# Band mask of the softmax maximum on VectorE, and the softmax reciprocals spread by DMA

## The chip, the cores and the metric

The kernel runs on one core of a Trainium2 chip. The profile calls the core's engines PE (TensorE, matmuls; PEld is its weight loads), DVE (VectorE), ACT (ScalarE), POOL (GpSimd) and SP (SyncE, which here issues almost every DMA). Each engine works through its own instruction list in order and waits on semaphores for the others. The metric is the device time of one execution in microseconds.

## The reference

Two independent results are computed and put side by side: a sliding-window attention on the left 576 columns, a long convolution (a state-space kernel, done by FFT) on the right 576.

```python
def _A_ref(x, wqkv, wo):                      # x: 1 x 2048 x 576
    H = 32; Dh = 18; W = 256
    q, k, v = ...                             # x @ wqkv, 32 heads of 18
    scores = jnp.einsum("bhqd,bhkd->bhqk", q, k) * (Dh ** -0.5)
    idx = jnp.arange(S)
    mask = (idx[:, None] - idx[None, :] >= 0) & (idx[:, None] - idx[None, :] < W)
    scores = jnp.where(mask[None, None], scores, -1e9)
    p = _softmax(scores, axis=-1)
    return (p @ v per head, heads joined) @ wo

def _B_ref(u, A_re, A_im, B_re, B_im, C_re, C_im, log_dt, Dskip):
    K = ...                                   # 576 kernels of length 2048 from 128 complex modes
    return causal_convolution(u, K) + u * Dskip
```

Only the attention's softmax is touched by the change.

## The kernel before

The program has three stages. Up to about 402 us the projections to q, k and v and the tables of the convolution's kernels are computed. From 402 to about 790 us the attention runs, with the convolution's spectra and inverse transforms mixed in. The rest is mostly the output projection.

The attention is cut into 16 *items*: four chunks of 512 queries by four groups of eight heads. An item passes through these steps, each a generator that yields its pieces:

- `smax`: for each of 8 blocks of 64 queries and two halves of the heads, a PSUM tile of 128 rows x 2 x 320 gets the scores of the block against the 320 keys that its window can touch (L836, four matmuls on the four quarters of the array). Four more matmuls (L844, or L847 where the window begins before the sequence does) multiply an identity by the constant `sm`, whose entries are 0 or -3e38, and so add the mask to the first and the last 64 keys. VectorE takes the maximum over each 320 (L870, one reduction of 128x640 to 128x2). Sixteen such tiles make an item's maxima; they are transposed (L852), halved to fp16 (L856) and stored by four small DMAs (L863, Q<-m) as an additional row of Q.
- `scores` computes the scores again with keys on the partitions, less the maximum (L921), masks them (L930), and ScalarE takes the exponential (L936).
- `pv` multiplies by V (L956). V carries a 19th column of constants, so that of each group of 32 partitions the rows 0 to 17 hold a head's output and row 18 holds the softmax's denominator. ScalarE copies the result to SBUF as `osb` (L966).
- `norm` turns row 18 into its reciprocal on all rows: VectorE transposes `osb` in 32x32 blocks (L981), takes the reciprocal of one column (L983), and transposes that column, repeated 32 times, back (L985). GpSimd multiplies (L990), ScalarE and GpSimd split the product into two fp16 parts (L994, L998), SyncE stores them (L1003, od<-oh). The output projection (L178) later reads them.

All tiles of TensorE in this stage, of attention and convolution alike (L675 and L708 are the convolution's spectra and inverse, L769 its last transform, L690 and L691 its products on VectorE), share a *ring* of three PSUM slots. A slot is free when the engine that reads the tile has finished.

The order of the work is written out by hand as a string, `PLAN`. A letter asks the generator of that name for its next piece (s for smax, a for scores, v for pv, n for norm, c and d for the convolution's spectra and inverse); a letter with a digit runs the oldest piece that the generator has posted under that digit, such as s2, the reduction of the oldest finished tile. The string sets the order on every engine at once, and on SyncE's queue.

## Time and profile before

| quantity | value |
|---|---|
| median of 3 runs | 883.62 us (881.54 to 885.16) |
| profiled execution: time | 884.13 us |
| profiled execution: span | 882.3 us |
| granted TensorE clock, mean | 0.922 |
| VectorE, maximum's reductions (L870) | 187.7 us in 256 instructions |
| VectorE, transposes (L981, L985), 16 each | 19.8 and 19.9 us |
| TensorE, mask matmuls of the maximum (L844, L847) | 56.9 and 6.8 us in 1024 instructions |

Times in the profile are microseconds from the start of the span unless they are marked ns. A row of the grouped view names line, engine, operation, output <- inputs, shapes and count, then the busy time, the mean length of one in ns, the engine's idle time just before, and which work ended that idle time. A row of the chain view is a start, a length and the work that held the path; it is followed back from the last instruction to what released it. A row of the waits view gives the total, the number and the longest of one kind of wait. The busy time of matmuls includes their passage through the array, so matmuls that overlap are counted by their union, and a busy TensorE need not be at its peak.

### The profile page before, as it was taken

The numbers are of one execution on the slowest core, as the hardware profiler recorded it, in microseconds if no ns is written. First come the engines' busy times: TensorE is split into PE (matmuls) and PEld (weight loads), VectorE is DVE, ScalarE is ACT, GpSimd is POOL, SyncE is SP. The second block draws the span as 40 slices with busy tenths as digits, with TensorE's granted clock in tenths as the row PEclk, the third lists the DMA queues.
The fourth block names the chain that finished last, engine by engine and source line by source line (L and its number), as shares of the span: only waits on it lengthen the run. The fifth ranks groups of instructions, "written<-read, shape, count | busy, mean of one in ns | idle before, by whom it ended". The sixth has DMA issues, their size and how long they took to land.

```text
span 882.3 us, 32024 instructions
## 1 busy us (share of the span) xinstructions
PE 724.2 (82%) x14234; PEld 440.0 (50%) x14234; DVE 599.7 (68%) x798; ACT 522.7 (59%) x685; POOL 378.0 (43%) x295
## 2 busy tenths in 40 slices
PE   4565957998889789886888888887998987999977
PEld 2321523456446545454555554455555554567655
DVE  5855887887987787768657796575876767861010
ACT  3247676678777857671455566555766666676421
POOL 2256867766687655665015142221332042432020
PEclk9885969999999999996889999869999999999998
DMA  9795261546247745458549667637639573846743
GB/s 310 256 230 137 61 160 34 141 100 175 63 106 199 152 116 161 99 158 233 145 147 293 212 212 232 163 103 240 204 120 270 166 227 116 264 144 181 236 143 129
DMA packets 211051, 150.85 MB, mean 171 GB/s; under 512 B 102698, under 2 KB 191530, under 8 KB 210656
## 3 DMA queue, kind: packets, MB, share of 16 engines
q1 hardware_dynamic: 208896, 144.80, 58.5%
q0 software_dynamic: 2016, 3.99, 1.5%
q8 instruction: 112, 1.84, 0.9%
q14 instruction: 27, 0.22, 0.1%
HBM read 83.50 MB, written 65.11 MB: 168 GB/s over the span
## 4 chain that ended last, share of the span: by engine, by line
PE 46%; DVE 17%; ACT 12%; issue 10%; DMA 6%; SPq 4%; POOL 4%; ACTq 0%; DVEq 0%; POOLq 0%
PE pp L178 9%; PE po L956 7%; PE ring L178 6%; DVE m L870 5%; ACT P L936 4%; PE ring L708 4%; PE ring L921 4%; PE ring L836 3%; PE ring L675 3%; PE ring L575 2%; PE ring L453 2%; PE ring L769 2%; PE ring L465 2%; DMA K<-kz 1%; DVE m L552 1%
## 5 line engine op out<-in xcount | busy, mean ns | idle before, releaser
L870 DVE TENSOR_REDUCE m<-ring 128x2 f32<-128x640 f32 (+4 forms) x256 | 187.7, 779 | 66.6 <-PE ring L844 61.5
L936 ACT ACTIVATE P<-ring,esc 128x1024 f32<-128x1024 f32 (+2 forms) x160 | 166.8, 1060 | 102.3 <-PE ring L930 91.7
L546 POOL TENSOR_TENSOR m<-A,tr 128x1024 f32<-128x1024 f32 x72 | 144.0, 2017 | 79.2 <-DVE m L552 66.7
L956 PE MATMUL po<-P,V 64*32 64x320 f32 (+4 forms) x2816 | 105.7, 369 | 6.3 <-issue 6.3
L836 PE MATMUL ring<-K,Q 54*64 54x320 f16 (+4 forms) x1024 | 82.3, 322 | 26.5 <-DMA K<-kz 8.6
L696 POOL TENSOR_TENSOR Y<-t,t 128x384 f32<-128x384 f32 x24 | 24.0, 998 | 139.2 <-DVE t L691 133.3
L990 POOL TENSOR_TENSOR osb<-osb,T 128x1024 f32<-128x1024 f32 x16 | 37.8, 2362 | 100.6 <-DVE T L985 80.9
L921 PE MATMUL ring<-Q,K 55*64 55x320 f16 (+4 forms) x1408 | 67.7, 270 | 14.1 <-ACT P L936 3.4
L836 PEld LDWEIGHTS <-Q 54*64 54x64 f16 x1024 | 42.8, 109 | 71.7 <-issue 63.4
L998 POOL TENSOR_TENSOR oh<-osb,oh 128x1024 f16<-128x1024 f32 x16 | 34.1, 2130 | 73.5 <-ACT oh L994 73.5
L178 PE MATMUL pp<-xh,wh 128*128 128x512 f16 x180 | 48.6, 401 | 19.0 <-ACT vst L365 9.6
L178 PEld LDWEIGHTS <-wh 128*128 128x128 f16 x324 | 31.7, 101 | 57.1 <-issue 17.6
L844 PE MATMUL ring<-sm,idb 64*64 64x128 bf16 x896 | 56.9, 229 | 1.5 <-issue 1.5
L552 DVE TENSOR_TENSOR m<-m,m 128x1024 f32<-128x1024 f32 x36 | 53.3, 1480 | 4.8 <-POOL m L546 4.7
L956 PEld LDWEIGHTS po<-P,V 64*32 64x32 f32 x2816 | 39.1, 108 | 34.5 <-issue 25.0
L575 PE MATMUL ring<-Q,m 128*32 128x64 f32 x2304 | 42.6, 231 | 16.1 <-DVE m L552 13.4
L921 PEld LDWEIGHTS <-K 55*64 55x64 f16 x1408 | 33.8, 110 | 42.7 <-issue 34.0
L575 PEld LDWEIGHTS ring<-Q,m 128*32 128x32 f32 x2304 | 37.0, 117 | 29.8 <-issue 12.6
L178 PE MATMUL pp<-xh,wl 128*128 128x512 f16 x180 | 49.9, 412 | 0.0
L981 DVE STREAM_TRANSPOSE T<-osb 128x1024 f32<-128x1024 f32 x16 | 19.8, 1235 | 42.7 <-ACT osb L966 42.7
L930 PE MATMUL ring<-tm,idb 64*64 64x128 bf16 (+1 forms) x1152 | 44.9, 213 | 2.9 <-issue 2.9
L527 POOL TENSOR_TENSOR tr<-tr,mab 128x768 f32<-128x768 f32 x18 | 33.6, 1867 | 31.2 <-ACT tr L522 31.1
(162 smaller groups left out, 1570.2 us busy)
## 6 DMA issues: line engine op xcount, KB each, us to landing
gx<-ust SPq DMA_DIRECT2D x16, 576.0 KB
gk<-kst SPq DMA_DIRECT2D x18, 512.0 KB
tx<-gx SPq DMA_DIRECT2D x24, 384.0 KB
tk<-gk SPq DMA_DIRECT2D x24, 384.0 KB
h<-ho SPq DMA_DIRECT2D x48, 192.0 KB
hp<-h SPq DMA_DIRECT2D x12, 768.0 KB
Q<-qz SPq DMA_DIRECT2D x16, 512.0 KB
K<-kz SPq DMA_DIRECT2D x16, 512.0 KB
```

Of the source, the lines that this page charges most:

```text
L178: self.nc.tensor.matmul(ps, u, v, start=(i == 0), stop=(i == len(ops) - 1))
L546: tt(m[part], A[:, ch, a0:a0 + 8].unsqueeze(3).to_broadcast(sh), tr[:, ch, part, 0:8].unsqueeze(2).to_broadcast(sh), op=OP.mult)
L552: self.nc.vector.tensor_tensor(m[0], m[0], m[1], op=OP.add)
L575: nc.tensor.matmul(kp[32 * st:32 * st + 32, j, :], m[:, ch, 32 * term:32 * term + 32], Q[:, ch, term, :], start=(term == 0), stop=(term == ...
L836: nc.tensor.matmul(ps[z:z + 64, b, :n], d["Q"][rr, 2 * b + pp, 64 * qb:64 * qb + 64], d["K"][rr, 2 * b + pp, k0:k1], start=True, stop=Fals ...
L844: nc.tensor.matmul(out, self.idb[rr], self.sm[rr], start=False, stop=True, skip_group_check=True)
L870: self.nc.vector.tensor_reduce(out, x, axis=AX.X, op=OP.max)
L921: nc.tensor.matmul(ps[z:z + 64, b, off:off + w], d["K"][rr, 2 * b + pp, kc:kc + 64], d["Q"][rr, 2 * b + pp, q0:q0 + w], start=(k == 0), st ...
L930: nc.tensor.matmul(ps[z:z + 64, b, 64 * blk:64 * blk + w], self.idb[rr], self.tm[rr, self.MO[kinds]:self.MO[kinds] + w], start=False, stop ...
L936: nc.scalar.activation(P[:, :, lo:hi], ps[:, :, lo:hi], AF.Exp, scale=self.esc)
L956: nc.tensor.matmul(po[32 * p:32 * p + 32, z, q0:q0 + w], V[64 * z:64 * z + 64, kb * 76 + 19 * p:kb * 76 + 19 * p + 32], P[p % 2][64 * z:64 ...
L990: nc.gpsimd.tensor_tensor(osb, osb, rb, op=OP.mult)
```

## The change

Two parts of the softmax are moved.

First, the mask of the maximum. The mask matmuls L844 and L847 are gone. The constant `sm` grows from 128 to 320 columns, with zeros in the middle, and VectorE adds it while it takes the maximum: per tile two passes over 320 elements in place of one reduction over 640. A pass writes the masked scores to a scratch tile that nothing reads, and a second instruction writes the accumulated maximum.

Second, the reciprocals of the items 0 to 13. A DMA takes row 18 of the four groups of `osb` into a 128x32 tile R (step n); VectorE takes its reciprocal (n5); a DMA stores it to DRAM (n7); four DMAs load it back, one row to 18 partitions each (n8), into one tile `rb` that all items share. GpSimd then multiplies as before (n3). Items 14 and 15 keep the transposes.

In `PLAN`, only steps of n are moved or added: n, which now issues a DMA, stands 1 to 98 steps earlier than the transposes stood; n5 comes 10 to 12 steps behind it, n7 two steps later, n8 seven or eight later still (18 once), and n3 where it was or, for four items, 7 to 38 steps later. All other letters keep their order.

```diff
-    sm = np.concatenate([np.where(x <= p, big, 0), np.where(x > p, big, 0)], 1)
+    sm = np.concatenate([np.where(x <= p, big, 0), np.zeros((64, 192)), np.where(x > p, big, 0)], 1)
...
-        "a1vc2asaa1a1s6Lavva1sc3aa1ss2s2svs2ss4saa1s2s2ssas2s2sa1kss2s2nvvn3aa1kcc1aa1dc2sad1s2sksvs2s2a1v1cc"
+        "a1nvc2asaa1a1s6Lavvn5a1sn7c3aa1ss2s2svn8s2ss4saa1s2s2ssas2s2sa1kss2s2vvn3aa1kcc1aa1dc2sad1s2sksvs2s2"
...
-        self.sm = ap.tile([128, 128], BF, name="sm")
+        self.sm = ap.tile([128, 320], BF, name="sm")
...
+        self.rden = self.p["dram"].tile([self.LR, 4, 1024], F32, name="rden")
+        self.rb = ap.tile([128, 1024], F32, name="rb")
+        nc.gpsimd.memset(self.rb, 1.0)
...
                         nc.tensor.matmul(ps[z:z + 64, b, :n], d["Q"][rr, 2 * b + pp, 64 * qb:64 * qb + 64],
-                                         d["K"][rr, 2 * b + pp, k0:k1], start=True, stop=False, skip_group_check=True)
-                for b in range(2):
-                    for r in range(2):
-                        z = 64 * (r ^ b)
-                        rr = slice(64 * r, 64 * r + 64)
-                        if full:
-                            out = ps[z:z + 64, b, :320].rearrange("p (t x) -> p t x", x=64)[:, 0:5:4]
-                            nc.tensor.matmul(out, self.idb[rr], self.sm[rr], start=False, stop=True,
-                                             skip_group_check=True)
-                        else:
-                            nc.tensor.matmul(ps[z:z + 64, b, n - 64:n], self.idb[rr], self.sm[rr, 64:],
-                                             start=False, stop=True, skip_group_check=True)
-                self.post("2", (ps,), lambda out=mv[:, :, 8 * pp + qb], x=ps[:, :, :n]: self.red(out, x))
+                                         d["K"][rr, 2 * b + pp, k0:k1], start=True, stop=True, skip_group_check=True)
+                self.post("2", (ps,), lambda s=8 * pp + qb, x=ps[:, :, :n], m=m: self.red(m, s, x))
...
-    def red(self, out, x):
-        self.nc.vector.tensor_reduce(out, x, axis=AX.X, op=OP.max)
+    def red(self, m, s, x):
+        n = x.shape[2]
+        for b in range(2):
+            y = self.p["m"].tile([128, 320], F32, name="masked")
+            self.nc.vector.tensor_tensor_reduce(y[:, :n], x[:, b], self.sm[:, 320 - n:], 1.0, -3e38, op0=OP.add, op1=OP.max,
+                                                accum_out=m[:, 16 * b + s:16 * b + s + 1])
         self.n["max"] += 1
...
+            R = np_.tile([128, 32], F32, name="R")
+            if i < self.LR:
+                nc.sync.dma_start(R, osb.rearrange("(p r) z (k c) -> r p (z k) c", r=32, c=32)[18])
+                self.post("5", (R,), lambda i=i, osb=osb, R=R: self.spread(i, osb, R))
+                continue
             T = np_.tile([128, 32, 32], F32, name="T")
             nc.vector.transpose(T.rearrange("p k r -> p (k r)"), osb.rearrange("p z c -> p (z c)"))
-            R = np_.tile([128, 32], F32, name="R")
...
+    LR = 14
+
+    def spread(self, i, osb, R):
+        nc, rb, row = self.nc, self.rb, self.rden[i]
+        nc.vector.reciprocal(R, R)
+
+        def out():
+            nc.sync.dma_start(row.rearrange("p (k c) -> (p k) c", c=32), R)
+            self.post("8", (R,), back)
+
+        def back():
+            for p in range(4):
+                nc.sync.dma_start(rb[32 * p:32 * p + 18], row[p:p + 1].partition_broadcast(18))
+            self.post("3", (rb,), lambda: self.norm2(i, osb, rb.rearrange("p (z c) -> p z c", z=2)))
+        self.post("7", (R,), out)
```

What the string does to two instruction lists. First VectorE around the reciprocal of item 3, in the kernel before. Names are output <- inputs; t are the convolution's products, and what stands in brackets is the counter that the instruction waits for (PE_49, DVE_49, Activation_49 and Pool_49 count finished instructions of an engine, DMAHW numbers finished DMAs).

```order
L870 TENSOR_REDUCE m<-ring 128x2 [waits PE_49] x7
L981 STREAM_TRANSPOSE T<-osb 128x1024 [waits Activation_49,Pool_49]
L983 RECIPROCAL R<-T 128x32 [waits DVE_49]
L985 STREAM_TRANSPOSE T<-R 128x1024 [waits DVE_49]
L690 TENSOR_TENSOR t_7204<-X,ring 128x768 [waits PE_49,Activation_49,Pool_49]
L691 TENSOR_TENSOR t_7205<-X,ring 128x768
L870 TENSOR_REDUCE m<-ring 128x2 [waits PE_49] x4
```

The same place in the changed kernel, whose lines are numbered otherwise: L864 are the new passes (`ISA` is a masked maximum, or with m alone the write of the accumulated value), L991 is the reciprocal.

```order
L864 ISA masked,m<-ring,sm 128x320 [waits DVE_49,PE_49]
L864 ISA m 128x1
L864 ISA masked,m<-ring,sm 128x320 [waits DVE_49]
L864 ISA m 128x1
L991 RECIPROCAL R<-R 128x32 [waits DMAHW4_49,DMAHW1_49]
L691 TENSOR_TENSOR t_7118<-X,ring 128x768 [waits PE_49,Activation_49,Pool_49]
L692 TENSOR_TENSOR t_7119<-X,ring 128x768
L864 ISA masked,m<-ring,sm 128x320 [waits DVE_49,PE_49]
```

The first four rows stand for one reduction of before. The reciprocal keeps its place behind the run of reductions and ahead of the products, but waits for a DMA in place of VectorE's own transpose.

Second, SyncE's queue where the loads of item 5 are issued (Q_4396, K_4397 and V_4398 are that item's tiles, od the stores of finished items, tx and tk loads of the convolution). Before:

```order
L721 DMA h<-ho 128x2x192 x2
L806 DMA Q_4396<-qz 128x2048
L807 DMA K_4397<-kz 128x4x512
L809 DMA K_4397<-kz 128x4x256
L812 DMA V_4398<-vd 128x912
L660 DMA tx<-gx 128x4x192
L660 DMA tk<-gk 128x4x192
```

In the changed kernel:

```order
L722 DMA h<-ho 128x2x192 x2
L977 DMA R<-osb 128x1x32
L994 DMA rden<-R 128x32
L810 DMA Q_4396<-qz 128x2048
L811 DMA K_4397<-kz 128x4x512
L813 DMA K_4397<-kz 128x4x256
L816 DMA V_4398<-vd 128x912
L999 DMA rb<-rden 18x1024 x4
L661 DMA tx<-gx 128x4x192
L661 DMA tk<-gk 128x4x192
```

Six DMAs of item 2 have come in between: the read of the denominators and the store of the reciprocals ahead of the next loads, the four broadcast loads behind them.

More of the change, by code (lines that the diff above doesn't have):

```diff
@@ new lines @@
+        "vd4a1sss2d1n8akva1sd4s2s2vd4asc3a1s2dslld1s6kn6ss4sas2s2svs2a1ss2savs2ss2a1sas2vd4a1sass2n3s2va1ss2s"
+        "as2n1vsa1as2n6a1ss2ss2vLcllv1c1aaa1a1vvc2nss2ss2fakva1aa1sn5fan7vss6a1c3ee1s2n8saa1s2dcd1e4vvc1c2aav"
+        "vc3a1sa1s2s4aasfvs2kla1a1slvs2v1Ln4n4cc1c2elnsve1vs2ss2asa1s2sn5aa1n7ss2ss2asn3s2n8a1ss2s2ss2ss2svva"
+        "lc3s2cn1lla1c1aa1ad4vvc2n3ssa1ss6as2s2a1vss2as4ssve4a1s2ss2avs2asa1a1ds2svad1s2a1n6ssc3s2s2sas2sv1a1"
+        "vvaas2a1a1nss2vvdss2d1asn5ss2n7s2a1fvkkLcn8c1d4c2vaa1dd1sss6n4s2ass2va1aa1n3ess2ve1ss4s2ss2avn1ss2a1"
@@ L128 @@
+        "ww1w4aaa1vva1ee1e4ee1faavva1n3w4a1aa1www1wwwww4wwvvw1w4fn1n6w1vvv1ee4nn3w1e1w4wn1ee1n4ww4www1w4wn6n4"
+        "wwww1w4w1wwww4e4e4ww1ww4w1wwwww4w1w4w1w4ww1w4",
 }
```

34 lines of the change are left out of this document (13 added, 21 removed).

## The prediction

> **What bounds the kernel now.** I read the page's busy shares first, then busy time by stage, then the chain of waits in the stage that the change touches, then who waits for whom there. All terms below are set against the profiled execution: span 882.3 us, time 884.13 us, which is 0.06% above the median of 883.62 us. About 0.5% (4.4 us) is what a measurement of this kernel can tell from no change.
>
> ```profile
> span 882.3 us, 32024 instructions
> PE 724.2 (82%) x14234; PEld 440.0 (50%) x14234; DVE 599.7 (68%) x798; ACT 522.7 (59%) x685; POOL 378.0 (43%) x295
> core 0: us, PE busy (x) PEld busy (x) DVE busy (x) ACT busy (x) POOL busy (x), PEclk, DMA share, GB/s
> 0.00:402.00 402.00, 310.71 (x3704) 176.68 (x3704) 308.04 (x407) 260.99 (x407) 253.38 (x212) 0.91 0.57 149
> 402.00:790.00 388.00, 333.15 (x9498) 205.83 (x9501) 284.19 (x383) 227.03 (x238) 109.20 (x76) 0.93 0.66 193
> 790.00:882.30 92.30, 80.30 (x1048) 57.45 (x1032) 7.51 (x8) 34.73 (x41) 15.43 (x9) 0.96 0.56 172
> ```
>
> The change lies almost wholly in the middle row: from 402 to 790 us TensorE is busy 333 of 388 us (86%), VectorE 284 (73%). Neither fills the stage alone. The chain of waits over the same stretch says what holds it:
>
> ```profile
> by line: PE po L956 14.1%; DVE m L870 11.2%; ACT P L936 9.8%; issue 9.0%; PE ring L921 7.7%; PE ring L708 7.7%; PE ring L836 7.6%; PE ring L675 6.3%; PE ring L769 3.6%; DMA K<-kz 3.3%; DMA Q<-m 2.5%; PE ring L930 2.4%; PE ring L844 2.0%; SP
> ```
>
> TensorE's lines in it add up to 51%, the maximum's reduction (L870) has 11.2% of 388, 43.5 us, and the mask matmuls that go (L844) have 2.0%, 7.8 us. The coupling is the ring of three PSUM slots: TensorE may begin a tile only when the engine that empties the tile three before has done so.
>
> ```profile
> 649.53 3.10 DVE L870 TENSOR_REDUCE m<-ring 128x2 f32<-128x640 f32 x4 [0.64 <-PE ring L844]
> 651.96 0.41 PE L921 MATMUL ring<-Q,K 55*64 55x320 f16 x8 [0.28 <-DVE m L870]
> 652.69 0.33 PE L836 MATMUL ring<-K,Q 54*64 54x320 f16 x4 [0.23 <-DVE m L870]
> DVE m L870 <- PE ring L844: 61.5, 66, 5.0
> ```
>
> Here four reductions run back to back, and two tiles of TensorE start as each of the last two frees a slot. The last row says that VectorE sat idle for a fresh tile only 66 times, 61.5 us in all; the other reductions found their tile ready. So a longer reduction is passed on to TensorE in bursts, and a shorter matmul helps between them.
>
> **The change, part by part.** Rows for the prices:
>
> ```profile
> L870 DVE TENSOR_REDUCE m<-ring 128x2 f32<-128x640 f32 x224 | 174.4, 821 | 63.0 <-PE ring L844 61.5
> L474 DVE TENSOR_TENSOR fa<-ring,fa 128x384 f32<-128x384 f32 x18 | 10.0, 553 | 17.7 <-ACT fa L471 17.7
> L474 DVE TENSOR_TENSOR fr<-ring,fr 128x512 f32<-128x512 f32 x36 | 24.7, 685 | 15.9 <-ACT fr L471 15.5
> L162 DVE TENSOR_SCALAR or<-or 128x1 f32<-128x1 f32 x1 | 0.2, 154 | 0.0
> L985 DVE STREAM_TRANSPOSE T<-R 128x1024 f32<-128x1024 f32 x14 | 17.4, 1245 | 0.5
> L981 DVE STREAM_TRANSPOSE T<-osb 128x1024 f32<-128x1024 f32 x14 | 17.3, 1233 | 0.0
> 717.66 0.06 PE ring L844 x4
> 649.43 0.08 PE ring L844 x4
> 717.77 4.56 DVE L870 TENSOR_REDUCE m<-ring 128x2 f32<-128x640 f32 x6 [4.97 <-PE ring L844]
> PE ring L836 <- DVE m L870: 3.9, 15, 0.4
> ```
>
> *A. 1024 mask matmuls and their weight loads go.* A step's four show 0.06 to 0.08 us on the chain (the rows at 717.66 and 649.43), since they follow the score matmuls in the pipeline. On the chain that is the 7.8 us above; I take −10 for the few that come beside it. Bounds: −4 (a slower VectorE hides half of it) and −20 (256 steps at 0.08).
>
> *B. One reduction of 128x640 becomes four VectorE instructions:* per half of the tile one add-and-maximum over 320 elements and one 128x1 write of the accumulated maximum. Neither is in the trace. The nearest row for the first is an addition that reads PSUM and SBUF: 685 for 512 elements, 553 for 384, so 132 ns for 128 elements and 553 − 66 = 487 ns for 320. The nearest for the second is the 128x1 row, 154 ns. Four together are 2 × (487 + 154) = 1.28 us. In a run the next instruction starts before the last has ended: six reductions in 4.56 us stand 0.75 apart ((4.56 − 0.82)/5), though each lasts 0.82, so 0.07 is won at each join. A write has to wait for its maximum, so I let only the joins behind the two writes overlap, 1.28 − 0.14 = 1.14, and set it against 0.75: +0.38 a step, rounded down. Bounds: every join overlaps, 1.00, and the new form is a little faster than the addition, +0.2; none does and it is a little slower, +0.55. The narrow steps of the first four items (32 of 256) change by about as much, because the fixed part dominates. On the path the 43.5 us are 43.5/0.75 = 58 reductions: 58 × 0.38 = +22 (bounds +12 and +32).
>
> The other 198 also grow. VectorE's load in the stretch becomes 284 + 256 × 0.38 − 35 (C) = 346 of 388, 89%; its idle time falls from 104 to 42 us, in scraps. What lay beside TensorE's work then comes onto the path in bursts like the one shown. No row prices this; it is 0 if all of it fits into idle time and +30 if half of the 61.5 us of waits above is lost too. I take +11, nearer the low end, since the waits of the score matmuls for a reduction are short today: 15, of 0.4 us at most (the last row).
>
> *C. 28 transposes go* (14 items, two each: 14 × (1.233 + 1.245) = 34.7 us of VectorE). The reciprocals stay. On the chain:
>
> ```profile
> 510.07 1.16 DVE T L981
> 511.64 0.49 DVE T L985
> 586.16 1.16 DVE T L981
> 587.73 0.86 DVE T L985
> 632.25 1.16 DVE T L981
> 633.83 0.36 DVE T L985
> 783.44 1.16 DVE T L981
> ```
>
> 4 × 1.16 + 0.49 + 0.86 + 0.36 = 6.4 us: −6 (0 if the work behind is late for another reason).
>
> *D. The reciprocal now waits for a small DMA*, and the convolution's products and the maxima stand behind it on VectorE; TensorE waits for these. How much time the DMA has is read from where the reciprocal now stands: in the tightest of the 14 places (item 3) after the run of seven reductions, in the widest (item 5) after a run of three.
>
> ```profile
> 516.30 1.02 ACT L966 ACTIVATE osb<-po 128x1024 f32<-128x1024 f32 x1
> 514.51 5.56 DVE L870 TENSOR_REDUCE m<-ring 128x2 f32<-128x640 f32 x7
> 567.11 1.03 ACT L966 ACTIVATE osb<-po 128x1024 f32<-128x1024 f32 x1 [1.52 <-PE po L956]
> 576.31 2.52 DVE L870 TENSOR_REDUCE m<-ring 128x2 f32<-128x640 f32 x3 [4.82 <-PE ring L844]
> 594.02 1.87 DMA Q<-m
> 740.63 4.02 DMA Q<-m
> 478.82 6.72 DMA K<-kz
> L1003 SPq DMA_DIRECT2D od<-oh x64: 264/316/1262, 489.9 to 848.3; - x64
> SPq L863 <- DVE m L856: 61.6, 11, 10.3
> ```
>
> From osb's end to the end of that run: 520.07 − 517.32 = 2.75 us for item 3, 578.83 − 568.14 less the third reduction (0.74) = 9.95 for item 5. Small transfers of the same kind (Q<-m, 128-byte pieces) took 1.87 to 4.02 us on the chain. So most places have time enough: +2, with 0 and +14 (a microsecond each) as bounds.
>
> *E. SyncE issues 84 more DMAs* (14 × 6). At the 0.316 us of the store's row that is 27 us of a queue that stands still for 61.6 us on one wait alone. But two of an item's steps wait in that in-order queue, the store of the reciprocals for VectorE and the four broadcast loads for the store's landing and for GpSimd's last multiplication; the next item's Q, K, V loads and the convolution's tx and tk loads are behind them. They are asked for about an item ahead (16 items in 388 us, 24 us each), so a delay of 2 to 4 us mostly stays hidden: +3, bounds 0 and +15. If that cover goes, the price is a transfer in the open, as the 6.72 us of the K load at 478.82.
>
> *F. 2048 fewer TensorE instructions* of 2 × 9,500 in the stretch, 11%; "issue" there is 9.0%, 35 us. If it goes with the count: −3 to −4; I take −3, bounds −7 and 0. GpSimd's multiplication stays where it was or slightly later, items 14 and 15 keep the transposes, and the last 92 us are left alone: 0. One memset of the spread tile is hidden in GpSimd's idle time.
>
> Sum: −10 + 22 + 11 − 6 + 2 + 3 − 3 = +19; 884.1 + 19 = 903 us. All low ends give −20 + 12 + 0 − 6 + 0 + 0 − 7 = −21 (863), all high ends −4 + 32 + 30 + 0 + 14 + 15 + 0 = +87 (971).
>
> **A rule against the change.** The Trainium skill, "VectorE: DVE Perf Modes", section "The DRAIN you can't avoid", says that a VectorE instruction begins only when the pipe of the one before is empty; the section "Two Vector instructions with no wait between them" exempts some without a wait, and counts an operation that writes out its accumulator as two instructions. The six reductions in 4.56 us agree with the exemption. The new passes each carry a wait on VectorE's own counter for their scratch tile; by the strict rule the four would cost 1.28 us, the second rival's price.
>
> **The rivals.**
> 1. *TensorE sets the pace and the new passes hide* (faster). Place: the steps between bursts. If the four instructions overlap at every join (+0.2), VectorE's load is 284 + 51 − 35 = 300, hardly more than now; B costs its +12 on the path, and all 256 steps lose 0.08: −20 + 12 − 6 − 3 = −17, 867 us. It decides below about 1.0 us for the four. For it: TensorE at 86%. Against it: only 7.8 us of masks on the chain.
> 2. *VectorE becomes the bound.* At 1.28 us or more the load is 284 + 256 × 0.52 to 0.55 − 35 = 382 to 390 of 388 us. If half of its present idle time, 52 us, still can't be filled: 386 + 52 − 388 = +50, 934 us. For it: the prices are those of whole instructions. Against it: the overlap in runs.
> 3. *The small DMAs land late.* If each of 14 reciprocals keeps VectorE waiting 2 us (a 4 to 5 us landing behind a busy SyncE queue), +28 in place of D's +2: 928. Against it: the budgets above.
> 4. *It evens out*: B nearly at its low end, +14 on the path and nothing beside it, against A, C and F (−19) and +5 of D and E: 884 us, give or take 4.
>
> **How the numbers follow.** My forecast, slower by about 19 us (888 to 921): 0.42. Rival 2 (921 to 960): 0.18. Rival 3: 0.08. Rival 4: 0.12. Rival 1 (855 to 879): 0.20. So faster 0.20, same 0.12, slower 0.68. The range 868 to 938 leaves out about half of rival 1 and a third of rival 2, not quite 2 in 10.
>
> **What would show it.** In the changed profile: a step's four VectorE instructions take 1.0 to 1.3 us from first start to last end; VectorE busy in the stage at 330 to 360 us; TensorE busy about 60 us less there (its own rows of the mask) without the span shrinking; more of TensorE's idle time, and of the chain, at the new maximum's line than 43.5 us; waits at the reciprocal of a few microseconds in all; SyncE's waits longer, but no DMA of Q, K or tx as a new large piece of the chain. The prediction is wrong if the pair of passes takes under 1.0 us, if VectorE stays below 80% with the chain on TensorE, or if the reciprocals' waits exceed 15 us.

## The result and the profile after

The changed kernel takes 933.41 us (median of 4 runs, 930.28 to 934.70) against 882.58 us (880.74 to 885.16) for the kernel before on the same chip: a ratio of 1.0567, with a 95% interval of 1.0517 to 1.0617. It is 51 us slower; 19 had been forecast. Line numbers in the rows of each kernel are its own.

The busy shares on the page of the changed kernel:

```profile
span 928.5 us, 31124 instructions
PE 726.9 (78%) x13210; PEld 422.9 (46%) x13210; DVE 589.3 (63%) x1538; ACT 522.3 (56%) x685; POOL 378.9 (41%) x296
```

Its stages. The columns are those of the same view shown of before: length, busy time of TensorE, its weight loads, VectorE, ScalarE and GpSimd, granted clock, DMA share and GB/s.

```profile
0.00:402.00 402.00, 312.54 (x3716) 177.21 (x3716) 310.98 (x408) 260.98 (x407) 253.42 (x213) 0.91 0.57 149
402.00:840.00 438.00, 337.38 (x8552) 190.70 (x8550) 272.64 (x1125) 228.44 (x240) 112.41 (x77) 0.86 0.64 183
840.00:928.50 88.50, 77.00 (x948) 54.98 (x945) 5.69 (x6) 32.91 (x39) 13.03 (x7) 0.95 0.55 170
```

The first 402 us and the end are nearly as they were (the border between the last two stages is set by eye, and the end comes out 4 us shorter). The loss is in the stage with the attention, which took 388 us and now takes 438. No engine has become its bound: VectorE, which was to be 89% busy, is busy 273 of 438 us (62%), less than the 284 us of before. The chain of waits over that stage names something else:

```profile
by line: PE po L951 10.6%; issue 10.3%; DVE masked L864 9.5%; PE ring L916 6.2%; PE ring L709 5.9%; PE ring L676 5.9%; ACT P L931 5.2%; PE ring L838 5.1%; DMA K<-kz 4.9%; DMA tk<-gk 3.3%; DMA h<-ho 3.2%; PE ring L770 2.8%; DMA V<-vd 2.6%; S
```

Loads of K, tk and V and the stores of h have 14%; before, K alone of these stood among the first on that line, with 3.3%. What kept them is in the waits of SyncE's queue from 402 to 890 us (which instruction stood, for whom, us in all, times, longest):

```profile
SPq L977 <- ACT osb L961: 37.2, 7, 9.1
SPq L999 <- DMA rden<-R: 27.7, 9, 7.1
SPq L994 <- DVE R L991: 19.5, 7, 5.3
SPq L994 <- DVE m L864: 16.6, 5, 5.8
SPq L854 <- DVE m L864: 17.4, 8, 8.2
```

L977 reads the denominators and stands for ScalarE's copy to `osb`; L994 stores the reciprocals and stands for VectorE, which is still at the reciprocal or at the maxima ahead of it; L999 loads them back and stands for the store's landing. Together they are 101 us in 28 waits. The last row is the store of the maxima, where SyncE had stood for 61.6 us before; so SyncE's standing is not new, but its place in the order is. What that does to the work behind shows best at one place. First SyncE's timeline from 631 us, then two rows of TensorE's, then the chain at the same place:

```profile
631.84 0.60 SPq L977 DMA_DIRECT2D R<-osb  x1
637.98 0.35 SPq L994 DMA_DIRECT2D rden<-R  x1
638.42 0.39 SPq L759 DMA_DIRECT2D hp<-h  x1
638.86 0.57 SPq L661 DMA_DIRECT2D tx<-gx  x1
639.49 0.50 SPq L661 DMA_DIRECT2D tk<-gk  x1
640.09 0.91 SPq L661 DMA_DIRECT2D tx<-gx  x1
641.10 1.08 SPq L661 DMA_DIRECT2D tk<-gk  x1
642.27 1.06 SPq L810 DMA_DIRECT2D Q<-qz  x1
643.38 0.59 SPq L811 DMA_DIRECT2D K<-kz  x1
644.03 0.90 SPq L813 DMA_DIRECT2D K<-kz  x1
```
```profile
644.59 1.53 PE L676 MATMUL ring<-tx,w 64*32 64x192 f32 x32 [5.92 <-DMA tx<-gx]
651.86 0.33 PE L838 MATMUL ring<-K,Q 54*64 54x320 f16 x4 [0.56 <-DMA K<-kz]
```
```profile
637.69 0.27 DVE R L991
...
643.38 7.48 DMA K<-kz
650.88 5.28 DMA h<-ho
```

From 632.44 to 637.98 SyncE issues nothing, because the store of the reciprocals stands at the head of its queue until VectorE has reached the reciprocal. The eight loads shown behind it need no reciprocal. They go out in a heap when it is over; TensorE waits 5.92 us for tx and 0.56 for K, and the path runs through the load of K.

### The profile page after: what moved, and what is told of

Its sections match the earlier page's. It is cut to its first block, busy times and chain, and to the rows that moved or that the text cites. A ratio compares the mean times of both kernels' runs of the same rounds, so it can differ in the third digit from the quotient of the medians.

```text
span 928.5 us, 31124 instructions
## 1 busy us (share of the span) xinstructions
PE 726.9 (78%) x13210; PEld 422.9 (46%) x13210; DVE 589.3 (63%) x1538; ACT 522.3 (56%) x685; POOL 378.9 (41%) x296
## 4 chain that ended last, share of the span: by engine, by line
PE 37%; DVE 17%; DMA 13%; ACT 11%; issue 11%; SPq 6%; POOL 3%; DVEq 0%; ACTq 0%; POOLq 0%
PE pp L179 7%; PE ring L179 6%; PE po L951 5%; DVE masked L864 4%; PE ring L916 3%; DMA K<-kz 3%; PE ring L709 3%; PE ring L676 3%; ACT P L931 3%; PE ring L838 2%; PE ring L770 2%; DMA tk<-gk 2%; PE ring L576 2%; DMA h<-ho 2%; DVE m L553 1%
## 5 line engine op out<-in xcount | busy, mean ns | idle before, releaser
L864 DVE CUSTOM_DVE_ANT_0 masked<-ring,sm 128x320 f32<-128x320 f32 (+4 forms) x512 | 207.9, 466 | 84.1 <-PE ring L838 83.2
L838 PE MATMUL ring<-K,Q 54*64 54x320 f16 (+4 forms) x1024 | 84.7, 344 | 51.6 <-DMA K<-kz 21.8
L916 PE MATMUL ring<-Q,K 55*64 55x320 f16 (+4 forms) x1408 | 71.5, 284 | 30.3 <-DMA Q<-m 9.6
L697 POOL TENSOR_TENSOR Y<-t,t 128x384 f32<-128x384 f32 x24 | 24.0, 1000 | 173.4 <-DVE t L692 140.1
L838 PEld LDWEIGHTS <-Q 54*64 54x64 f16 x1024 | 31.9, 112 | 106.4 <-issue 58.9
L1005 POOL TENSOR_TENSOR osb<-osb,rb 128x1024 f32<-128x1024 f32 x14 | 33.0, 2358 | 103.5 <-DMA h<-ho 42.3
L691 DVE TENSOR_TENSOR t<-X,ring 128x768 f32<-128x768 f32 x24 | 22.9, 954 | 58.5 <-PE ring L676 30.8
L488 ACT ACTIVATE ring<-ring 128x1024 f32<-128x1024 f32 x36 | 36.7, 1018 | 12.9 <-PE ring L466 10.9
```

Source lines behind the costliest of these rows:

```text
L488: self.nc.scalar.activation(m, m, AF.Exp)
L838: nc.tensor.matmul(ps[z:z + 64, b, :n], d["Q"][rr, 2 * b + pp, 64 * qb:64 * qb + 64], d["K"][rr, 2 * b + pp, k0:k1], start=True, stop=True ...
L864: self.nc.vector.tensor_tensor_reduce(y[:, :n], x[:, b], self.sm[:, 320 - n:], 1.0, -3e38, op0=OP.add, op1=OP.max, accum_out=m[:, 16 * b + ...
L916: nc.tensor.matmul(ps[z:z + 64, b, off:off + w], d["K"][rr, 2 * b + pp, kc:kc + 64], d["Q"][rr, 2 * b + pp, q0:q0 + w], start=(k == 0), st ...
```

## The experiments

They first split the change into its two parts, then the spread into its DMAs and their waits, then ask whether it is SyncE that matters, and last take the mask apart. Theory Q says that the cost is what the spread's waits do to the work behind them in SyncE's queue. Its rivals are M, the passes on VectorE; T, the DMAs' own issue and traffic; and the late data for themselves, whatever queue waits. Ratios are to the kernel before on the same chip; 1% is 8.8 us.

### Each part alone

The mask on VectorE without the spread: `LR = 0` and the plan of before.

```diff
-    LR = 14
+    LR = 0
...
-        self.rden = self.p["dram"].tile([self.LR, 4, 1024], F32, name="rden")
-        self.rb = ap.tile([128, 1024], F32, name="rb")
-        nc.gpsimd.memset(self.rb, 1.0)
```

> The mask on VectorE alone; the transposes and the order of before. Theory Q (the cost is what the spread's DMAs do to SyncE's queue): a step costs VectorE 0.08 us more, 58 of them on the chain +5, the masks give back 8 to 20, so 865 to 885 us, and the waits for K, V and tk are as before. Theory M (the passes on VectorE are the cost, and the late DMAs only follow from a later softmax): 905 us or more, with the DMA pieces of the chain still there.

Measured: 1.0012 (0.9973 to 1.0051), 884.5 us. Then the spread without the new mask, that is `sm`, `smax1` and `red` of before in the changed kernel:

```diff
-            self.nc.vector.tensor_tensor_reduce(y[:, :n], x[:, b], self.sm[:, 320 - n:], 1.0, -3e38, op0=OP.add, op1=OP.max,
-                                                accum_out=m[:, 16 * b + s:16 * b + s + 1])
+        self.nc.vector.tensor_reduce(out, x, axis=AX.X, op=OP.max)
```

> The spread by DMAs and the changed order alone; the mask by TensorE and one reduction as before. Theory Q: 930 to 945 us, the changed kernel's time plus the masks that TensorE keeps, and the new DMA pieces of the chain (K, V, tk, h) as in the changed kernel. Theory M: 880 to 900 us.

Measured: 1.0560 (1.0504 to 1.0617), 932.3 us. The first part costs nothing that can be told from no change; the second is the whole loss, and the two add up to that of the changed kernel. Theory M falls.

### The DMAs without their waits, and without the DMAs

In this kernel the 84 DMAs stay in SyncE's queue with their sizes and places, but move constants.

```diff
-                nc.sync.dma_start(R, osb.rearrange("(p r) z (k c) -> r p (z k) c", r=32, c=32)[18])
+                nc.sync.dma_start(R, self.one.rearrange("p (z c) -> p z c", z=2).rearrange("(p r) z (k c) -> r p (z k) c", r=32, c=32)[18])
...
-            nc.sync.dma_start(row.rearrange("p (k c) -> (p k) c", c=32), R)
+            nc.sync.dma_start(row.rearrange("p (k c) -> (p k) c", c=32), self.one[:, :32])
...
-                nc.sync.dma_start(rb[32 * p:32 * p + 18], row[p:p + 1].partition_broadcast(18))
+                nc.sync.dma_start(rb[32 * p:32 * p + 18], self.a["u2"].rearrange("a b d -> a (b d)")[p:p + 1, :1024].partition_broadcast(18))
-            self.post("3", (rb,), lambda: self.norm2(i, osb, rb.rearrange("p (z c) -> p z c", z=2)))
+            self.post("3", (rb,), lambda: self.norm2(i, osb, self.one.rearrange("p (z c) -> p z c", z=2)))
```

> The changed kernel with the same 84 DMAs in the same places, sizes and queue, but cut from the data: the read takes a constant tile, the store stores a constant, the broadcast loads take an input, and GpSimd multiplies by a constant tile (so the output isn't normalized). SyncE no longer waits for ScalarE, VectorE, the store's landing or GpSimd at these DMAs. Theory Q in its narrow form (the waits in SyncE's in-order queue are the cost): 862 to 882 us. Theory T (the DMAs' own traffic and issue time are the cost): 915 us or more. In between the two share it.

Measured: 1.0122 (1.0084 to 1.0160), 891.9 us. Most of the loss goes with the waits, 1.0567 − 1.0122 = 4.45 points or 39 us; but it didn't fall to the 882 us that the narrow form of theory Q allowed at most. The chain by engine over the whole span, of the changed kernel and then of this one:

```profile
PE 37%; DVE 17%; DMA 13%; ACT 11%; issue 11%; SPq 6%; POOL 3%; DVEq 0%; ACTq 0%; POOLq 0%
```
```profile
PE 39%; DVE 17%; DMA 15%; ACT 12%; issue 11%; SPq 4%; POOL 2%; DVEq 0%; ACTq 0%; POOLq 0%
```

DMAs have as much of the path here as there, at 42 us less: their pieces on the chain show where the path runs, not what the change costs. That had to be measured by leaving things out. The next kernel leaves the 84 DMAs out as well, and takes the reciprocal of a constant:

```diff
-                nc.sync.dma_start(R, self.one.rearrange("p (z c) -> p z c", z=2).rearrange("(p r) z (k c) -> r p (z k) c", r=32, c=32)[18])
...
-        nc.vector.reciprocal(R, R)
+        nc.vector.reciprocal(R, self.one[:, :32])
...
-            nc.sync.dma_start(row.rearrange("p (k c) -> (p k) c", c=32), self.one[:, :32])
...
-            for p in range(4):
-                nc.sync.dma_start(rb[32 * p:32 * p + 18], ...)
```

> The kernel cut from the data, with its 84 DMAs left out: VectorE takes the reciprocal of a constant tile, GpSimd multiplies by a constant (the output isn't normalized). What is left against the mask alone (1.0012) is the loss of the 28 transposes: by term C -6, so 874 to 880 us. Against the kernel with the DMAs but without their waits (1.0122) it gives the price of issuing and moving them: 84 x 0.31 us of SyncE, 10 us if a third of it shows. If the two are equal, traffic and issue cost nothing and that 1.2% comes from the changed order.

Measured: 0.9956 (0.9918 to 0.9995), 879.9 us. So the DMAs without waits cost 1.66 points, some 15 us, more than the 10 expected; the transposes' loss against the mask alone is 0.56 points, 5 us, though its uncertainty (about 0.55, from the two intervals) nearly reaches zero. In one more kernel the broadcast loads move 32 columns in place of 1024:

```diff
-                nc.sync.dma_start(rb[32 * p:32 * p + 18], self.a["u2"].rearrange("a b d -> a (b d)")[p:p + 1, :1024].partition_broadcast(18))
+                nc.sync.dma_start(rb[32 * p:32 * p + 18, :32], self.a["u2"].rearrange("a b d -> a (b d)")[p:p + 1, :32].partition_broadcast(18))
```

> The kernel cut from the data, with the same 84 DMAs in the same places, but the broadcast loads move 32 columns in place of 1024 (0.13 of 4.1 MB; their tile isn't read, and the output isn't normalized). With the loads whole it took 1.0122 of the kernel before, without all 84 DMAs 0.9956. If the bytes are the price: 0.996 to 1.003, 879 to 886 us. If it is the issue of 84 more DMAs in SyncE's queue: 1.009 to 1.013, 891 to 895 us.

Measured: 1.0067 (1.0017 to 1.0116). It lies between the two answers, and its interval reaches into both: how the 15 us divide into issue and bytes stays open. VectorE, too, still waits 14.4 us in the kernel cut from the data, for the read of the constant to land; that such a wait of VectorE costs little here is shown at the end of the next group.

### Which wait

Starting from the kernel cut from the data, one wait at a time is put back.

```diff
-                nc.sync.dma_start(R, self.one.rearrange("p (z c) -> p z c", z=2).rearrange("(p r) z (k c) -> r p (z k) c", r=32, c=32)[18])
+                nc.sync.dma_start(R, osb.rearrange("(p r) z (k c) -> r p (z k) c", r=32, c=32)[18])
```

> The kernel cut from the data (891.9 us), with one of the waits put back: the read takes osb and so waits in SyncE's queue for ScalarE. If each of the three waits does its share of the 41.5 us between 891.9 and 933.4, 901 to 909 us. If the read's wait, which comes first and is the longest in the changed kernel (37.2 us), is nearly all of it, 920 us or more. If it only makes the later waits shorter, 890 to 896. (As there, the output isn't normalized by the sums.)

Measured: 1.0287 (1.0222 to 1.0352), 915.5 us: 1.65 points for the read's wait, about 15 us.

```diff
-            nc.sync.dma_start(row.rearrange("p (k c) -> (p k) c", c=32), self.one[:, :32])
+            nc.sync.dma_start(row.rearrange("p (k c) -> (p k) c", c=32), R)
```

> The kernel cut from the data, with the second wait put back alone: the store takes R and waits in SyncE's queue for VectorE's reciprocal. Equal shares: 901 to 909 us. This wait alone nearly all: 920 or more. None of it: 889 to 895. (The output isn't normalized.)

Measured: 1.0383 (1.0305 to 1.0460), 920.2 us: 2.6 points for the store's wait, about 23 us. Nothing reads what this store writes, so what can be late is what stands behind it in the queue. VectorE's wait at the reciprocal did not grow with it: 12.7 us, against 14.4 without the store's wait.

```diff
-                nc.sync.dma_start(rb[32 * p:32 * p + 18], self.a["u2"].rearrange("a b d -> a (b d)")[p:p + 1, :1024].partition_broadcast(18))
+                nc.sync.dma_start(rb[32 * p:32 * p + 18], row[p:p + 1].partition_broadcast(18))
...
-            self.post("3", (rb,), lambda: self.norm2(i, osb, self.one.rearrange("p (z c) -> p z c", z=2)))
+            self.post("3", (rb,), lambda: self.norm2(i, osb, rb.rearrange("p (z c) -> p z c", z=2)))
```

> The kernel cut from the data, with the third wait put back alone: the broadcast loads take the stored row and fill the tile that GpSimd multiplies by, so they wait in SyncE's queue for the store's landing and for GpSimd's multiplication of the item before, and GpSimd waits for them. Equal shares: 901 to 909 us. This wait alone nearly all: 920 or more. None of it: 889 to 895. (What is stored is a constant, so the output isn't normalized.)

Measured: 1.0104 (1.0042 to 1.0166), 896.3 us: nothing that can be told, although SyncE stands there as well and GpSimd's product comes later. Two rows from 402 to 890 us of this kernel, of SyncE's queue and of GpSimd:

```profile
SPq L1001 <- DMA rden<-one: 30.2, 10, 5.4
POOL osb L1007 <- DMA rb<-rden: 29.0, 3, 15.6
```

Shares are not equal, then, and none of the three times fell into the 901 to 909 us of equal ones: read 1.65, store 2.6, loads −0.2, in sum 4.1 of the 4.45 points, each with an uncertainty of 0.7 to 0.9 points from the two intervals. The read and the store stand ahead of the next item's Q, K and V loads, the broadcast loads behind them (in SyncE's order, shown with the change); that this is why they cost nothing is argued, not shown.

The read's wait had also kept VectorE, whose reciprocal took what was read. The last kernel of this group takes that away:

```diff
-                self.post("5", (R,), lambda i=i, osb=osb, R=R: self.spread(i, osb, R))
+                self.post("5", (), lambda i=i, osb=osb, R=R: self.spread(i, osb, R))
...
-        nc.vector.reciprocal(R, R)
+        nc.vector.reciprocal(self.rec, self.one[:, :32])
```

> The kernel cut from the data with the read of osb put back, but nothing uses what it reads: the reciprocal takes a constant tile, so VectorE waits for no DMA. The read alone with VectorE's wait gave 1.0287, neither 1.0122. Theory Q (the wait in SyncE's queue for itself, through the loads and stores behind it): 1.022 to 1.032, 902 to 913 us. If it was VectorE's wait for the late read: 1.010 to 1.016, 892 to 898 us.

Measured: 1.0276 (1.0198 to 1.0353), 907.2 us. Nobody needs these 14 reads, and they cost what they did with a user. Of its profile, SyncE's wait from 402 to 890 us and two rows of the chain:

```profile
SPq L980 <- ACT osb L964: 38.2, 8, 8.6
```
```profile
619.55 8.96 DMA K<-kz
...
696.32 8.55 DMA tk<-gk
```

So 38 us of standing in the queue become some 14 us of time, give or take 8. The Trainium skill, "DMA: Bandwidth & Descriptors", section "Anatomy of one DMA — SWDGE (gpsimd) path", notes, where it describes the DMAs of GpSimd, that a DMA engine waits for no semaphore itself and that the wait is held by the sequencer that issues it. This trace agrees for a DMA of SyncE: it is SyncE that stands, for 38.2 us, and the loads behind it.

### Does it have to be SyncE's queue?

All 84 DMAs issued by GpSimd, first with real data, then cut from the data:

```diff
-                nc.sync.dma_start(R, osb.rearrange("(p r) z (k c) -> r p (z k) c", r=32, c=32)[18])
+                nc.gpsimd.dma_start(R, osb.rearrange("(p r) z (k c) -> r p (z k) c", r=32, c=32)[18])
...
-            nc.sync.dma_start(row.rearrange("p (k c) -> (p k) c", c=32), R)
+            nc.gpsimd.dma_start(row.rearrange("p (k c) -> (p k) c", c=32), R)
...
-                nc.sync.dma_start(rb[32 * p:32 * p + 18], row[p:p + 1].partition_broadcast(18))
+                nc.gpsimd.dma_start(rb[32 * p:32 * p + 18], row[p:p + 1].partition_broadcast(18))
```

> The changed kernel with the 84 DMAs issued by GpSimd in place of SyncE, at the same places of the order. Theory Q: SyncE's loads and stores are no longer behind these waits, while GpSimd, busy a quarter of the stage, takes them; 870 to 900 us. Theory T, or a cost that lies in the length of the path from denominators to the product: 920 us or more.

> The kernel cut from the data with its 84 DMAs issued by GpSimd in place of SyncE (the output isn't normalized). With real data GpSimd's issuing gave 1.0273. If the waits are the price there too: 0.996 to 1.008, 879 to 890 us, and the rest up to 1.027 is what they cost in GpSimd's queue. If GpSimd's issuing of 84 DMAs is itself the price: 1.018 or more, 899 us.

Measured: 1.0273 (1.0221 to 1.0324), 906.5 us, with real data; 1.0039 (1.0000 to 1.0078), 889.2 us, without. With real data it lies between the two answers: SyncE's waits for the spread are gone, and half of the loss with them; but the waits cost 2.3 points in GpSimd's queue too. Two of GpSimd's rows from 402 to 890 us, with real data:

```profile
POOL rb L999 <- DMA rden<-R: 38.1, 11, 5.5
POOL osb L1005 <- DMA rb<-rden: 21.4, 8, 6.4
```

Next the read from ScalarE, right behind its own copy, the store from GpSimd, the loads still from SyncE:

```diff
-                nc.sync.dma_start(R, osb.rearrange("(p r) z (k c) -> r p (z k) c", r=32, c=32)[18])
+                nc.scalar.dma_start(R, osb.rearrange("(p r) z (k c) -> r p (z k) c", r=32, c=32)[18])
...
-            nc.sync.dma_start(row.rearrange("p (k c) -> (p k) c", c=32), R)
+            nc.gpsimd.dma_start(row.rearrange("p (k c) -> (p k) c", c=32), R)
```

> The changed kernel with the read issued by ScalarE, right behind its own copy to osb, and the store by GpSimd; the broadcast loads stay with SyncE. Theory Q: the two waits that cost 15 and 23 us in SyncE's queue are gone from it, the third costs nothing there, so 890 to 900 us, with GpSimd's wait for the reciprocal and ScalarE's issue time as the price. If the cost follows the data (late reciprocals, late products) and not the queue: 915 us or more.

Measured: 1.0364 (1.0288 to 1.0440), 915.3 us, a miss. SyncE had not been freed; its row from 402 to 890 us:

```profile
SPq L999 <- DMA rden<-R: 83.7, 11, 11.1
```

The loads that stayed behind now wait for a store that itself waits in GpSimd's queue: 27.7 us of standing have become 83.7. GpSimd, too, stands 80.7 us for the reciprocals, with the convolution's sums behind it. Which of the two makes the loss is not separated, and the time is also one that the rival, late data whatever the queue, had named.

Then the queue as it was, but the spread's steps later in the plan (of item 0, read 13 steps later, reciprocal 14, store and loads 21; the letters around them keep their order):

```diff
-"a1nvc2asaa1a1s6Lavvn5a1sn7c3aa1ss2s2svn8s2ss4saa1s2s2ssas2s2sa1kss2s2vvn3"
+"a1vc2asaa1a1s6Lavva1nsc3aa1ss2s2svs2ss4sn5aa1s2s2ssas2s2n7sa1kss2s2vvn8n3"
```

> The changed kernel with the read, the reciprocal, the store and the loads of each item 13 to 24 steps later in the plan (loads at the latest just ahead of GpSimd's multiplication), all in SyncE's queue as before. Theory Q: SyncE finds osb and the reciprocal ready more often, so half or more of the 41 us comes back, 895 to 915 us, and what is left is GpSimd's wait for late loads. If it isn't when SyncE gets to them that matters: 925 us or more.

Measured: 1.0356 (1.0311 to 1.0401), 913.8 us: 2.1 of the 5.7 points come back, in the range but just under the half of the 41 us that theory Q had asked for. SyncE's rows from 402 to 890 us, and GpSimd's:

```profile
SPq L994 <- DVE R L991: 18.6, 4, 7.9
SPq L977 <- ACT osb L961: 17.9, 6, 6.4
SPq L999 <- DMA rden<-R: 17.7, 10, 3.6
SPq L994 <- DVE m L864: 9.7, 5, 3.1
SPq L994 <- DVE m L847: 6.7, 1, 6.7
POOL osb L1005 <- DMA rb<-rden: 84.3, 9, 20.7
```

71 us of standing in place of 101; what was won may in part have been paid by GpSimd, which waits 84.3 us for the loads that come later (42.2 in the changed kernel). Both at once, the later plan with the read from ScalarE and the rest from GpSimd:

```diff
-                nc.sync.dma_start(R, osb.rearrange(...)[18])
+                nc.scalar.dma_start(R, osb.rearrange(...)[18])
...
-            nc.sync.dma_start(row.rearrange("p (k c) -> (p k) c", c=32), R)
+            nc.gpsimd.dma_start(row.rearrange("p (k c) -> (p k) c", c=32), R)
...
-                nc.sync.dma_start(rb[32 * p:32 * p + 18], row[p:p + 1].partition_broadcast(18))
+                nc.gpsimd.dma_start(rb[32 * p:32 * p + 18], row[p:p + 1].partition_broadcast(18))
```

> The changed kernel with real data, none of the 84 DMAs in SyncE's queue, and the later plan: the read issued by ScalarE behind its own copy, the store and the loads by GpSimd 18 to 24 steps later. Theory Q, with the misses taken in (a wait moved to another queue is paid for there too): SyncE's waits and its share of issue time are gone, and the later steps leave GpSimd less to wait for, so below the 1.027 of the kernel with all 84 issued by GpSimd: 1.005 to 1.02, 888 to 901 us. If the lateness of the product for itself is the cost, whatever the queue: as the two other variants, 1.03 or more.

Measured: 1.0383 (1.0294 to 1.0473), 915.3 us, a miss, at what the rival of theory Q had named. GpSimd from 402 to 890 us, and the chain from 402 to 840 us:

```profile
POOL rden L994 <- DVE R L991: 58.7, 7, 16.9
POOL osb L1005 <- DMA rb<-rden: 44.3, 10, 11.2
POOL rb L999 <- DMA rden<-R: 33.5, 12, 5.6
```
```profile
by line: issue 11.4%; DMA rb<-rden 8.9%; PE po L951 7.6%; ACT P L931 6.1%; DVE masked L864 6.0%; DMA rden<-R 5.9%; PE ring L916 5.1%; PE ring L709 4.7%; PE ring L676 4.6%; PE ring L838 3.6%; POOL osb L1005 3.3%; DMA od<-oh 2.9%; POOL rb L99
```

137 us of standing in GpSimd's queue, with the convolution's sums (L697, L698) and the next products behind it. The loads are on time here: TensorE's matmuls wait 2.3 us in all for transfers over that stretch. The path runs through the spread's own store and loads instead, which have 15% of it. So theory Q holds in a wider form only: in the changed kernel the cost is in SyncE's queue, but GpSimd's queue paid as well where it carried the chain of waits. How much of what is left here is the queue and how much the later product is not separated.

### The mask taken apart

The kernel before without its mask matmuls and with nothing in their place, so that the maximum is taken over masked scores too:

```diff
-                                         d["K"][rr, 2 * b + pp, k0:k1], start=True, stop=False, skip_group_check=True)
-                for b in range(2):
-                    for r in range(2):
...
-                            nc.tensor.matmul(out, self.idb[rr], self.sm[rr], start=False, stop=True,
-                                             skip_group_check=True)
...
+                                         d["K"][rr, 2 * b + pp, k0:k1], start=True, stop=True, skip_group_check=True)
```

> The kernel before without the maximum's mask matmuls and with nothing in their place: terms A and F of the prediction alone (the maximum is then taken over masked scores too). By the prediction's price: 10 and 3 us less, 864 to 876 us. If the masks hide in TensorE's pipeline behind the score matmuls, as their 0.06 to 0.08 us a step on the chain may mean, or if a faster TensorE only waits more: 879 to 887.

Measured: 0.9806 (0.9769 to 0.9844), 871.0 us: 17 us less, inside the first answer. What is subtracted before the exponential cancels in the quotient, so a maximum over more scores does for these inputs; where a masked score lies far above all others it could make a row's exponentials vanish. With that limit it is faster than both kernels.

Next the passes with the mask matmuls kept. The passes add zeros, from columns added behind `sm`:

```diff
+                for b in range(2):
+                    for r in range(2):
...
+                            nc.tensor.matmul(out, self.idb[rr], self.sm[rr, 0:320].rearrange("p (t x) -> p t x", x=64)[:, 0:5:4],
+                                             start=False, stop=True, skip_group_check=True)
...
-            self.nc.vector.tensor_tensor_reduce(y[:, :n], x[:, b], self.sm[:, 320 - n:], 1.0, -3e38, op0=OP.add, op1=OP.max,
+            self.nc.vector.tensor_tensor_reduce(y[:, :n], x[:, b], self.sm[:, 640 - n:], 1.0, -3e38, op0=OP.add, op1=OP.max,
```

> The kernel before with its mask matmuls kept and the two passes on VectorE put in place of the reduction (they add zeros): term B of the prediction alone. The two runs with and without the passes (1.0012 and 0.9806 of the kernel before) differ by 2.1 points; if B costs that whatever TensorE does, 1.02, or 897 to 906 us. If it is dearer in a stage where TensorE is the later one, more; if the passes then hide behind TensorE, 884 to 892 us. By the prediction's price it would be 33 us, 915 us.

Measured: 1.0080 (1.0046 to 1.0114), 891.2 us. So with the masks kept the passes hide for the most part, at the upper end of the 884 to 892 us named for that. The passes cost 0.8 points, 7 us, while TensorE keeps its masks, and 1.0012 − 0.9806 = 2.1 points, 18 us, without them. The mask on VectorE gains 17 us on TensorE and loses 18 on VectorE.

## Why the prediction was wrong

The account in points of the time before, each the difference of two kernels: mask matmuls gone −1.9, passes +2.1, transposes gone −0.6, 84 DMAs without their waits +1.7, their waits +4.45; in sum +5.7, or +50 us. The kernels form one row from before to after, so the sum comes out by construction, and a price can depend on the place in the row, as that of the passes does. What checks it are the two parts alone, 0.1 + 5.6, and the waits put back one at a time, 4.1 of the 4.45.

**B, the four VectorE instructions, was priced too high** (+33 us; measured 7 to 18). The rows of the changed kernel from 402 to 840 us, grouped by shape, and two of VectorE's timeline:

```profile
L864 DVE CUSTOM_DVE_ANT_0 masked<-ring,sm 128x320 f32<-128x320 f32 x448 | 191.3, 487 | 78.2 <-PE ring L838 77.6
L864 DVE DVE_READ_ACCUMULATOR2_ANT m<- 128x1 f32 x512 | 42.6, 83 | 0.0
```
```profile
690.02 0.08 DVE L864 DVE_READ_ACCUMULATOR2_ANT m<- 128x1 f32 x1
690.02 0.49 DVE L864 CUSTOM_DVE_ANT_0 masked<-ring,sm 128x320 f32<-128x320 f32 x1
690.43 0.08 DVE L864 DVE_READ_ACCUMULATOR2_ANT m<- 128x1 f32 x1
690.43 0.49 DVE L864 CUSTOM_DVE_ANT_0 masked<-ring,sm 128x320 f32<-128x320 f32 x1
```

A pass takes 487 ns, as estimated. The write takes 83, not 154, and begins with the pass behind it; passes stand 0.41 us apart. A step takes 2 × 0.41 = 0.83 us in a run against 0.75: +0.08, not +0.38. The step of the working that failed is "a write has to wait for its maximum": the write is as late as said, but it keeps nothing behind it. By the strict form of the rule that the prediction cites (the Trainium skill, "VectorE: DVE Perf Modes", section "The DRAIN you can't avoid") it would have been 1.28 us, an estimate; the passes' wait on VectorE's own counter didn't bring that on here. Why the passes still cost up to 18 us shows in the chain of the kernel with the mask alone, from 402 to 790 us:

```profile
by line: issue 14.9%; DVE masked L860 13.7%; PE po L947 11.9%; PE ring L912 7.5%; PE ring L675 6.6%; PE ring L834 6.4%; PE ring L708 5.6%; ACT P L927 4.8%; PE ring L769 3.2%; DVE m L860 2.7%; DVE t L691 2.5%; PE ring L921 2.5%; DVE t L690 2
```

The maximum has 16.4% of 388 us there, 64 us, 20 more than before: 64/0.83 = 77 steps instead of 58 are on the path, each a little longer. With the masks kept on TensorE as well, the passes and writes have 9.6% of the same stretch, 37 us. So a faster TensorE waits for VectorE more often, and the gain of A goes there.

**A and F** were right: −13 forecast, −17 measured, inside their bounds. **C** fits: −6 forecast, −5 measured, with an uncertainty as large. So of the mask's sum, A, B and F, +20 was forecast and 1 us measured, and the difference is nearly all in B.

**E, SyncE's queue, is the step that failed and the cause of the result**: +3 forecast with a bound of +15, and +2 for D; measured 15 us for the DMAs and 39 for their waits. The waiting steps were named, and what stands behind them; wrong was "so a delay of 2 to 4 us mostly stays hidden". The single waits were longer, up to 9.1 us at the read, there were 28 of them in the first four rows of SyncE's waits above, and the loads behind go out in a heap, each later than the one before. TensorE's own wait for K, before (402 to 790 us) and after (402 to 840):

```profile
PE ring L836 <- DMA K<-kz: 8.6, 2, 8.4
PE ring L838 <- DMA K<-kz: 14.7, 5, 7.4
```

All its waits for K, Q's added row, tx, tk and hp went from 12.1 to 34.2 us. With the DMAs cut from the data they are 11.3, and with the store's wait put back alone 27.7. The rest of the loss is not assigned to single waits. "No DMA of Q, K or tx as a new large piece of the chain" was wrong for K. The case that was named as the price of lost cover, a K load of 6.72 us in the open, is what came: 7.48 us at 643.38.

**D** stayed inside its bounds: the reciprocals keep VectorE idle for 10.8 us from 402 to 890 us, where 14 us at most was forecast, and the idle time made no difference to the time that could be seen (1.0287 with such a wait, 1.0276 without).

```profile
DVE R L991 <- DMA R<-osb: 10.8, 3, 9.6
```

Of the rivals, 3 gave nearly the measured time (928), by the wrong mechanism: VectorE's waits were 10.8 us, not 28. Rival 2 fell, with VectorE at 62%. Rival 1's condition was met, the four under 1.0 us, and its 867 us still not reached when the DMAs were left out (0.9956); by the account above, the growth of B on the path ate it. Rival 4 describes the mask part well (1.0012), not the whole.

One of the prediction's own signs of being wrong came, the four instructions under 1.0 us, and half of another, VectorE below 80%, but without the chain on TensorE. The forecast had the right sign, and its range, up to 938, held the time, but that was luck: its 19 us were made of the wrong term, B's +33 in place of E's. With the mask's sum as measured and D and E as forecast it would have been no change at all (1 − 6 + 2 + 3 = 0).

## What to carry to other kernels

Count a small DMA by what stands behind it in its queue, not by its bytes: each DMA that waits for an engine holds up every later load of that queue, and 14 reads that nobody used cost some 14 us. A chain of three dependent DMAs per item through an in-order queue can pay at each link, here at two of the three, and moving a link to another queue moves the wait with it; look at whose work stands behind there, and whether the link that stays now waits longer. An instruction that follows on another's result, like the write of an accumulator, need not delay the one behind it: price a run by starts, not by lengths.

## What had not been expected of the hardware

Taking 1024 mask matmuls away, whose rows add up to 63.7 us, lowered TensorE's busy time by 12 us only, on the page of the kernel without any mask:

```profile
PE 712.6 (82%) x13210; PEld 420.8 (48%) x13210; DVE 600.1 (69%) x798; ACT 522.4 (60%) x685; POOL 377.9 (43%) x295
```

In the changed kernel it even rose, from 724.2 to 726.9 us, at a granted clock of 0.889 in place of 0.922, where 60 less had been forecast for the stage. The time of the kernel without a mask still fell by 17 us, so neither the sum of the rows nor the busy time said what they cost.

The granted clock of the stage fell with the waits, in one profiled execution each, of kernels with the same TensorE work. From 402 to 790 us, a stretch of the stage with the attention, in order: without the DMAs, with the DMAs cut from the data, and with the store's wait put back:

```profile
402.00:790.00 388.00, 329.39 (x8749) 189.74 (x8750) 270.29 (x1102) 235.45 (x248) 113.65 (x79) 0.92 0.66 193
```
```profile
402.00:790.00 388.00, 316.08 (x8350) 179.67 (x8346) 268.36 (x1118) 224.15 (x235) 107.32 (x74) 0.90 0.71 202
```
```profile
402.00:790.00 388.00, 303.01 (x7653) 169.33 (x7653) 248.78 (x1038) 206.48 (x217) 100.39 (x68) 0.86 0.66 189
```

One wait more, and the clock is 0.86 in place of 0.90. Over the whole stage of each kernel, to 780, 799 and 828 us, it is 0.92, 0.90 and 0.87, and TensorE is busy 320, 324 and 336 us there with the same work. Over all executions the medians of the whole span's clock are 0.91, 0.91 and 0.89. How much of that wait's 23 us is the waiting and how much the slower matmuls after it isn't separated.
